# F in tiles of 64x64 instead of 32x32, its blocks put in order by the copies, in an RWKV-7 and feed-forward kernel

## The chip, the cores and the metric

The kernel runs on one core of a Trainium2 chip. The metric is the device time of one execution in microseconds; the time before is the median of eight runs, 871.92 us (868.44 to 874.09). Lower is better. Engines are named as in the profile: PE (TensorE matmul), PEld (its weight loads), DVE (VectorE), ACT (ScalarE), POOL (GpSimd), SP (SyncE, which issues nearly all DMAs). Times "at 289.78" are microseconds from the start of the profiled execution's span, and L450 is line 450 of the kernel.

## What is computed

Two blocks, one after the other, in fp32. The first is a recurrence over 768 tokens for 4 batches x 8 heads, with a 40 x 40 state for each; the second is a feed-forward layer over the 3072 resulting rows:

```python
for t in range(S):                       # r, k, v, w, a, b: (4, 8, 768, 40)
    y[:, :, t] = np.einsum('bhd,bhde->bhe', rt, state)
    Sa = np.einsum('bhde,bhe->bhd', state, at)
    state_decay = state * wt[:, :, None, :] - np.einsum('bhd,bhe->bhde', Sa, bt)
    state = state_decay + np.einsum('bhd,bhe->bhde', vt, kt)
x = y.transpose(0, 2, 1, 3).reshape(3072, 320)
h = x @ w_in                             # 320 -> 2048
out = (h * np.clip(h + 3.0, 0.0, 6.0) / 6.0) @ w_out
```

## The kernel before, in words

**Units.** The recurrence is worked off in blocks of 64 tokens. A unit is one such block for two batches (two halves of 64 partitions, `q`) and all eight heads (four pairs `pr` of two heads `s`). There are 24 units; four of them (`NU`) make a group. A unit's work is split into stages, each a small generator: first it issues matmuls or transposes on PE, then yields, then issues what reads the PSUM result.

**Stages that prepare a unit** (`prepare`, L389): W (decay, L391, then the scan on DVE), gam (reciprocals and copies of the running products), A and B (transposes of a and b, scaled into `at` and `bt`), F (L438, the products of `at` and `bt` within the block), K, factor (L458: four transposes of the decay on PE, the ACT copy `rgt` at L465, two POOL products `KBt` at L473), E (products of `kt` and `at`) and EV. **Stages that carry the state** (`step`, L594): RT, VT, S (transposes), R (L619, at times state), U (L653), UT (L674), rS (L690), C, sn (L708), H, y (L731), move.

**F and the inversion.** F holds, for each batch and head, a 64 x 64 matrix of which two 32 x 32 diagonal blocks and one off-diagonal block are used. It is written per unit to a tile for the whole group (`F`, 128 partitions x 32 heads x 64). The lower 32 rows of each half hold their two column blocks in exchanged order, so that both diagonal blocks lie in columns 0 to 31. When the group's fourth unit has its F (units 7, 11, 15, 19, 23), `invert` (L526) begins: one DVE transpose `fb` (L531) of columns 0 to 31 of the whole group, a masking on POOL (`x`, L534), then 30 pairs of DVE instructions (L543 and L549, forward substitution), two DVE transposes (L552, L556) and copies to `tinv`. It is handed out in small steps between other work (`aside`). `third_block` (L565) then makes the off-diagonal blocks from rows 32 to 63 and columns 32 to 63 of F, two units at a time.

**F's two steps before.** PE: 32 matmuls with 32 columns of weights (40 x 32) and 64 columns of data, each placed on an array tile of 64 rows x 32 columns; for the lower rows (`c` = 1) the data are read with exchanged halves. ACT: two copies of 128 partitions x 256 elements with factor -1 (L456). A matmul in fp32 is two records in the profile, so F shows as 64.

**PSUM.** The recurrence has a ring of five banks of 128 x 512 (`any`); `ps_any` takes the next one, and a pair of results (`ps_pair`, one for each `s`) takes two, which later stages share while columns are left. The feed-forward part has two banks `h` and one `o`. A bank is taken again only when all that reads it has been done.

**The order of the work** is written out by hand; each engine runs its queue in that order. From unit 4 on, the main loop (L1062) goes through four blocks per unit. `a_block` (L1031) collects the stages due in a block: those of the unit that carries the state (`OWN_STAGES`) and those of units being prepared ahead (`AHEAD_STAGES`, or `CLOSE_STAGES` where the next unit begins less than four blocks later, as in units 8 to 11; there, factor stands in the same block as F, otherwise one block later). `begins` (L1028) sets when units are begun: unit 8 in block 0, then 9, 10 and 11 three blocks apart, from 12 on four apart. `together` (L998) issues the PE parts of the collected stages in the order `PRODUCTS` (factor early, F last) as long as five banks suffice, then the parts that read them in the order `RESULTS`, in which F stands ahead of factor. Between the two halves of a block, `feed` gives out pieces of the feed-forward stream: `expand` (L806 and L811 on PE, relu on ACT at L816, the product `gt` on DVE at L817) and `contract` (L830 on PE, the output copy `ob` at L848).

Of the kernel before, what the change touches and what calls it, by code (L numbers as in the profile page):

```python
# [12 lines left out]
AF = mybir.ActivationFunctionType  # L13
# [3 lines left out]
P = 128  # L17
BL = 64
HB = BL // 2
L = 32  # L20
# [3 lines left out]
def _ap(ap, extra, dims):  # L24

    return bass.AP(tensor=ap.tensor, offset=ap.offset + extra, ap=[list(ap.ap[0])] + dims)
# [3 lines left out]
def kernel(  # L30
# [42 lines left out]
    nc = tc.nc  # L73
    B, H, T, D = r.shape
    NG = T // (2 * BL)
    NPR = H // 2
    NP = B // 2
    NU = 2 * NP
# [21 lines left out]
    def ps_any(shape):  # L100
        tag, bufs = ring[0]
        ring.rotate(-1)
        return bank(tag, shape, bufs)
# [4 lines left out]
    def ps_pair(*dims):  # L108

        n = 1  # L110
        for d in dims:
            n *= d
        if shared[0] is None or shared[1] + n > 512:
            shared[:] = [ps_any([P, 512]) for _ in range(2)], 0
        at = shared[1]
        shared[1] += n
        views, step = [], n
        for d in dims:
            step //= d
            views.append([step, d])  # L120
        return [_ap(t[:], at, views) for t in shared[0]]
# [6 lines left out]
        out=ident[:], in_=ones, pattern=[[1, P]],  # L128
# [4 lines left out]
        out=ones[:, 0:BL], in_=ones[:, 0:BL], pattern=[[1, BL]],  # L133
# [3 lines left out]
        out=ones[BL:P, 0:BL], in_=ones[BL:P, BL:P], pattern=[[1, BL]],  # L137
# [34 lines left out]
    start = const.tile([P, SCAN], F32, name="start")  # L172
# [12 lines left out]
    for i in range(3):  # L185
        t = const.tile([P, H, BL], F32, name=f"score{i}")
# [14 lines left out]
    for p in range(NP):  # L201
        t = const.tile([P, 2, NPR, SLOT], F32, name=f"state{p}")
        nc.vector.memset(t[:], 0.0)
        state.append(t)
        t = const.tile([P, 2, NPR], F32, name=f"last{p}")
# [113 lines left out]
    PE, DONE = 1, 2  # L319
# [46 lines left out]
    def half(i, n=SLOT):  # L366
        return slice(SLOT * i, SLOT * i + n)
# [21 lines left out]
    def prepare(i, F):  # L389
        n, o = i % NU, data[i]  # L390
# [44 lines left out]
            bt = o["bt"] = turned("bt")  # L435
            nc.vector.tensor_tensor(out=bt[:], in0=x[:], in1=o["rg"][:], op=ALU.mult)

        def f_stage():  # L438

            f = ps_pair(NPR, BL)  # L440
            for pr in range(NPR):
                for c in range(2):
                    for q in range(2):
                        for s in range(2):
                            x = q * BL + c * L
                            y = o["bt"][half(s, D), pr, half(q)].rearrange("p (c t) -> p c t", c=2)
                            if c:
                                y = y[:, ::-1, :]
                            z = (q ^ s) * BL + c * L
                            nc.tensor.matmul(out=f[s][z:z + L, pr, :],  # L450
                                             lhsT=o["at"][half(s, D), pr, x:x + L], rhs=y,
                                             start=True, stop=True, tile_position=(s * SLOT, z))
            yield PE
            for s in range(2):
                x = n * H + 4 * s
                nc.scalar.activation(out=F[:, x:x + 4, :], in_=f[s], func=AF.Copy, scale=-1.0)  # L456

        def factor_stage():  # L458

            rg = ps_any([P, NPR, P])  # L460
            for pr in range(NPR):
                nc.tensor.transpose(out=rg[:, pr, :], in_=o["rg"][:, pr, :], identity=ident[:])
            yield PE
            rgt = tmp.tile([P, H, D], F32, name="rgt", bufs=RGT)
            nc.scalar.activation(  # L465
                out=rgt[:], in_=rg[:].rearrange("p r (s e) -> p (r s) e", s=2)[:, :, 0:D],
                func=AF.Copy,
            )
            t = grp.tile([P, HD + WPAD], F32, name="KBt", tag="KBt", bufs=NU + 2)
            nc.gpsimd.memset(t[:, 2 * HD:], 0.0)  # L470
            for x, name in enumerate("KB"):
                o[name] = t[:, x * HD:x * HD + WPAD]
                nc.gpsimd.tensor_tensor(  # L473
                    out=o[name][:, 0:HD].rearrange("p (h e) -> p h e", h=H),
                    in0=o[name + "N"][:, :, 0:D], in1=rgt[:], op=ALU.mult,
                )
            if i > 2 * NU:
                fetch("V", i)
            for name in "BK":
                fetch(name, following(i))  # L480
# [12 lines left out]
        def ev_stage():  # L493
# [10 lines left out]
            for q in range(2):  # L504
                for s in range(2):
                    nc.scalar.activation(out=EV[half(q ^ s), s], in_=ev[q][half(q ^ s)], func=AF.Copy)
            o["EV"] = EV

        return {"W": w_stage, "gam": gam_stage, "A": a_stage, "B": b_stage, "F": f_stage,
                "factor": factor_stage, "K": k_stage, "E": e_stage, "EV": ev_stage}  # L510

    def in_turn(stages, order):
# [375 lines left out]
    third, F, group_F = [], None, []  # L888

    def prepared(i):  # L890
        nonlocal F
        if i >= NK:
            return None
        if i % NU == 0:
            F = inv.tile([P, NH, BL], F32, name="F", tag="F", bufs=2)
            group_F.append(F)
        return prepare(i, F)
# [223 lines left out]
```

## Time and profile before

| | |
|---|---|
| median of 8 runs | 871.92 us (868.44 to 874.09) |
| the profiled execution | 871.94 us, of which its span 870.2 |
| mean granted PE clock | 0.932 of full speed |
| PE busy, of 870.2 | 787.3 us |
| DVE, ACT, POOL busy | 535.7, 288.8, 150.9 us |
| F's matmuls, L450 | 1536 records, 64 in each unit |
| F's copies, L456 | 48, 390 ns each (median) |

The last 1.7 us of the profiled execution's time lie outside the span. In the profile's time lines a row gives the start, the length from the first start to the last end, the engine, line, operation, output <- inputs, the shape, and how many instructions were merged into the row; in brackets stand the engine's idle time ahead of it and the releaser, where there is one. Because matmuls overlap, the pace of PE is read from the start of one row to the start of the next. The profile's stretches give busy time per engine between two times, and the granted clock (1.00 is full speed).

### The profile page before, as it was taken

The numbers are of one execution on the slowest core, as the hardware profiler recorded it, in microseconds if no ns is written. First come the engines' busy times: TensorE is split into PE (matmuls) and PEld (weight loads), VectorE is DVE, ScalarE is ACT, GpSimd is POOL, SyncE is SP. The second block draws the span as 40 slices with busy tenths as digits, with TensorE's granted clock in tenths as the row PEclk, the third lists the DMA queues.
The fourth block names the chain that finished last, engine by engine and source line by source line (L and its number), as shares of the span: only waits on it lengthen the run. The fifth ranks groups of instructions, "written<-read, shape, count | busy, mean of one in ns | idle before, by whom it ended". The sixth has DMA issues, their size and how long they took to land.

```text
span 870.2 us, 36251 instructions
## 1 busy us (share of the span) xinstructions
PE 787.3 (90%) x16128; PEld 671.3 (77%) x16128; DVE 535.7 (62%) x1141; ACT 288.8 (33%) x694; POOL 150.9 (17%) x295
## 2 busy tenths in 40 slices
PE   4710988798999999999999999999999999999998
PEld 3610876686888788887888888788888888888886
DVE  7999678878845579833679543787445774221211
ACT  1334744232333322432323433223342224322211
POOL 4221011122111130220221122112212202000000
PEclk8655568998999999999999999999999999999999
DMA  6543434431122331322221232221232101110000
GB/s 132 89 109 94 114 105 106 71 65 33 30 50 52 62 56 30 56 44 40 50 49 37 46 53 51 39 51 31 46 59 42 26 19 27 22 24 13 18 17 15
DMA packets 175979, 45.08 MB, mean 52 GB/s; under 512 B 157904, under 2 KB 173264, under 8 KB 175824
## 3 DMA queue, kind: packets, MB, share of 16 engines
q1 hardware_dynamic: 174768, 42.61, 25.2%
q8 instruction: 127, 2.08, 1.0%
q10 hardware_dynamic: 1056, 0.16, 0.1%
q14 instruction: 28, 0.23, 0.1%
HBM read 34.08 MB, written 3.93 MB: 44 GB/s over the span
## 4 chain that ended last, share of the span: by engine, by line
PE 69%; DVE 6%; issue 2%; SPq 2%; ACT 1%; POOL 1%; DMA 0%; DVEq 0%
PE o L830 22%; PE h L806 18%; PE h L811 5%; PE any L358 5%; PE any L376 3%; PE any L708 2%; PE any L731 2%; PE any L450 2%; DVE x L549 1%; DVE prod L543 1%; PE any L619 1%; PE any L584 1%; PE any L653 1%; PE any L572 1%; PE any L690 1%
## 5 line engine op out<-in xcount | busy, mean ns | idle before, releaser
L830 PE MATMUL o<-wout,gt 128*128 128x320 f32 x768 | 232.4, 448 | 0.8 <-issue 0.6
L806 PE MATMUL h<-xt,win 128*128 128x128 f32 x1536 | 196.8, 281 | 0.6 <-DVE gt L817 0.6
L806 PEld LDWEIGHTS h<-xt,win 128*128 128x128 f32 x1536 | 185.0, 194 | 10.5 <-DVE gt L817 1.4
L830 PEld LDWEIGHTS o<-wout,gt 128*128 128x128 f32 x768 | 140.0, 191 | 56.0 <-issue 2.5
L817 DVE SCALAR_TENSOR_TENSOR gt<-gt,h 128x512 f32<-128x512 f32 x96 | 61.5, 682 | 110.5 <-ACT gt L816 110.5
L816 ACT ACTIVATE gt<-h,three 128x512 f32<-128x512 f32 x96 | 60.8, 685 | 159.5 <-PE h L811 159.4
L741 POOL TENSOR_TENSOR yg<-ys,gam 128x512 f32<-128x512 f32 x24 | 41.4, 1724 | 220.8 <-DVE ys L738 148.3
L543 DVE TENSOR_TENSOR prod<-x 128x30 f32<-128x30 f32 (+9 forms) x180 | 63.5, 353 | 11.7 <-POOL x L534 6.9
L549 DVE TENSOR_TENSOR x<-x,prod 128x30 f32<-128x30 f32 (+9 forms) x180 | 63.0, 350 | 4.3
L473 POOL TENSOR_TENSOR KBt<-K,rgt 128x320 f32<-128x320 f32 x24 | 22.4, 935 | 222.3 <-ACT rgt L465 208.6
L811 PE MATMUL h<-xt,win 64*128 64x128 f32 x768 | 56.2, 286 | 0.0
L385 DVE COPY_PREDICATED score<-mask,any 128x256 f32<-128x256 int32 x143 | 53.0, 434 | 0.0
L811 PEld LDWEIGHTS h<-xt,win 64*128 64x128 f32 x768 | 47.0, 188 | 5.4 <-issue 0.4
L412 DVE RECIPROCAL gam<-prods 128x256 f32<-128x256 f32 x24 | 41.4, 1739 | 13.4 <-POOL yg L741 13.1
L738 DVE TENSOR_TENSOR ys<-any,ys 128x256 f32<-128x256 f32 x48 | 18.2, 420 | 45.5 <-PE any L500 29.3
L715 DVE TENSOR_TENSOR state<-any,state 128x160 f32<-128x160 f32 x48 | 13.2, 316 | 49.6 <-PE any L376 49.4
L427 DVE RECIPROCAL rgam<-prods 128x256 f32<-128x256 f32 x24 | 41.8, 1741 | 0.0
L401 DVE TENSOR_TENSOR_SCAN prods<-wm,start 128x528 f32<-128x528 f32 x24 | 30.1, 1254 | 17.1 <-ACT wm L398 15.5
L572 PE MATMUL any<-tb,F 32*32 32x32 f32 x768 | 16.0, 199 | 26.7 <-DVE tb L552 26.3
L267 ACT ACTIVATE parts<-parts,low 128x256 uint32<-128x256 uint32 x40 | 20.3, 508 | 56.8 <-DVE parts L265 56.6
L572 PEld LDWEIGHTS any<-tb,F 32*32 32x32 f32 x768 | 14.6, 115 | 29.5 <-issue 27.9
L605 ACT ACTIVATE RT<-any 128x512 f32<-128x512 f32 x24 | 14.3, 596 | 65.9 <-PE any L358 65.9
(136 smaller groups left out, 1181.7 us busy)
## 6 DMA issues: line engine op xcount, KB each, us to landing
raw<-in_moe_w_out_dram SPq DMA_DIRECT2D x20, 256.0 KB
B<-in_b_dram SPq DMA_DIRECT2D x48, 80.0 KB
K<-in_k_dram SPq DMA_DIRECT2D x48, 80.0 KB
V<-in_v_dram SPq DMA_DIRECT2D x96, 40.0 KB
R<-in_r_dram SPq DMA_DIRECT2D x96, 40.0 KB
out_dram<-ob SPq DMA_DIRECT2D x48, 80.0 KB
W<-in_w_dram SPq DMA_DIRECT2D x40, 80.0 KB
A<-in_a_dram SPq DMA_DIRECT2D x40, 80.0 KB
```

Of the source, the lines that this page charges most:

```text
L358: nc.tensor.transpose(out=o[:, n, :], in_=x[:, 2 * n:2 * n + 2, :].rearrange("p s e -> p (s e)"), identity=ident[:])
L385: nc.vector.copy_predicated(out=x[:, 4 * i:4 * i + 4, :], mask=mask4, data=o[i])
L412: nc.vector.reciprocal(gv[:, :, 0:HB], o["prods"][:, :, 0, 1:HB + 1][:, :, ::-1])
L427: nc.vector.reciprocal(rv[:, :, HB:BL], o["prods"][:, :, 1, 1:HB + 1])
L543: nc.vector.tensor_tensor(out=pv, in0=_ap(x[:], (i + 1) * L + i, [[L, n], [0, i]]), in1=_ap(x[:], i * L, [[0, n], [1, i]]), op=ALU.mult,)
L549: nc.vector.tensor_tensor(out=rest, in0=rest, in1=pv, op=ALU.add)
L741: nc.gpsimd.tensor_tensor(out=yg[:], in0=m["ys"][:].rearrange("p r q t -> p r (q t)"), in1=o["G"][:], op=ALU.mult)
L806: nc.tensor.matmul(out=hp[c][:, i, :], lhsT=win[:, t, j * P:(j + 1) * P], rhs=xt[:, t, :], start=(t == 0 and i == 0), stop=False)
L811: nc.tensor.matmul(out=hp[c][:, i, :], lhsT=win2[half(c), (j0 + i) * P:(j0 + i + 1) * P], rhs=xt[half(c), 2, :], start=False, stop=(i == N ...
L816: nc.scalar.activation(out=gt[:], in_=hp[c][:], func=AF.Relu, bias=three[:], scale=1.0)
L817: nc.vector.scalar_tensor_tensor(out=gt[:], in0=gt[:], scalar=6.0, in1=hp[c][:], op0=ALU.min, op1=ALU.mult)
L830: nc.tensor.matmul(out=op[:], lhsT=gts[c][:, n, :], rhs=wout[:, c * HJ + r * NQ + n, :], start=((split or r == 0) and c == 0 and n == 0), ...
```

## The change

From the ninth unit on (units 8 to 23, `i >= 2 * NU`) F is made by 16 matmuls with 64 columns of weights on array tiles of 64 x 64, with the data read in their own order. The exchange of the lower rows' column blocks is done by the copies instead: for each `s` and each half, one copy of the upper 32 rows, columns 0 to 31 only (32 partitions x 128 elements), and one of the lower 32 rows with the two blocks of 32 columns exchanged (32 partitions x 256 elements). So the two copies become eight. Columns 32 to 63 of the upper rows are no longer written; nothing reads them. Units 0 to 7 keep the old form, now called `f_by_32`.

```diff
-        def f_stage():
+        def f_by_32():
...
+        def f_by_64():
+
+            f = ps_pair(NPR, BL)
+            for pr in range(NPR):
+                for q in range(2):
+                    for s in range(2):
+                        nc.tensor.matmul(out=f[s][half(q ^ s), pr, :],
+                                         lhsT=o["at"][half(s, D), pr, half(q)],
+                                         rhs=o["bt"][half(s, D), pr, half(q)],
+                                         start=True, stop=True)
+            yield PE
+            for s in range(2):
+                x = n * H + 4 * s
+                for z in range(0, P, BL):
+                    nc.scalar.activation(out=F[z:z + L, x:x + 4, 0:L], in_=f[s][z:z + L, :, 0:L],
+                                         func=AF.Copy, scale=-1.0)
+                    y = f[s][z + L:z + BL].rearrange("p r (c t) -> p r c t", c=2)
+                    nc.scalar.activation(
+                        out=F[z + L:z + BL, x:x + 4, :].rearrange("p h (c t) -> p h c t", c=2),
+                        in_=y[:, :, ::-1, :], func=AF.Copy, scale=-1.0)
...
-        return {"W": w_stage, "gam": gam_stage, "A": a_stage, "B": b_stage, "F": f_stage,
+        return {"W": w_stage, "gam": gam_stage, "A": a_stage, "B": b_stage, "F": f_by_32 if i < 2 * NU else f_by_64,
```

## The prediction

> **What bounds the kernel now.** I read the page first (busy shares, then the chain that ended last), then busy time by stretches, then the instructions in order of time around the sixteen F stages that change.
>
> ```profile
> PE 787.3 (90%) x16128; PEld 671.3 (77%) x16128; DVE 535.7 (62%) x1141; ACT 288.8 (33%) x694; POOL 150.9 (17%) x295
> ...
> PE 69%; DVE 6%; issue 2%; SPq 2%; ACT 1%; POOL 1%; DMA 0%; DVEq 0%
> ```
>
> The chain is mostly TensorE (PE), so PE time taken away is time gained, wherever PE doesn't wait. The stretches say where that is (columns: stretch, its length, then busy us of PE, PEld, DVE, ACT and POOL, granted clock, DMA):
>
> ```profile
> 244.00:356.00 112.00, 109.01 (x2510) 92.55 (x2507) 74.29 (x146) 36.66 (x93) 22.61 (x44) 1.00 0.29 51
> 356.00:870.00 514.00, 506.75 (x10208) 432.69 (x10208) 258.05 (x527) 160.09 (x375) 80.04 (x141) 1.00 0.19 36
> ```
>
> The changed units 8 to 23 have their F matmuls (L450) at 247.7, 269.3, 288.9, 308.6 and 335.8 (units 8 to 12) and from 369.6 to 676.1 (units 13 to 23). From 356 on PE has hardly any idle time, and the chain is PE throughout. From 316 to 356 the chain runs through VectorE (DVE): the first of the later inversions is pressed into that time, and PE waits for DVE at 324.41 (0.77 us) and at 356.00 (0.42 us). So a gain of PE counts in units 8 to 11 (unless a new wait eats it) and 13 to 23, and is worth nothing in unit 12.
>
> **What the matmuls give.** F goes from 32 matmuls of 32 columns of weights to 16 of 64 (each is two records, 64 and 32). The same shape runs in E and H (L376) and in rS (L690), so its price is in the trace; unit 15, PE alone:
>
> ```profile
> 425.41 0.67 PE L674 MATMUL any<-tinv,RR 64*64 64x64 f32 x32
> 425.90 0.65 PE L690 MATMUL any<-RT,S 40*64 40x64 f32 x32
> 426.48 0.86 PE L450 MATMUL any<-bt,at 40*32 40x64 f32 x64
> 427.27 2.42 PE L830 MATMUL o<-wout,gt 128*128 128x320 f32 x8
> ...
> 436.31 0.65 PE L376 MATMUL any<-at,kt 40*64 40x64 f32 x32
> 436.89 0.54 PE L830 MATMUL o<-wout,gt 128*128 128x320 f32 x1
> ```
>
> Start to start, a 64-wide block takes 0.49 us before another 64-wide one (425.41 to 425.90) and 0.58 before a change of shape (L690 to L450, L376 to L830); L450 takes 0.79. After rS (units 8 and 12 to 23), L690 and L450 cost 0.58 + 0.79 now and 0.49 + 0.58 then: 0.29 us less (1.37 - 1.07, by unrounded starts). In units 9 to 11 L450 follows 128-wide transposes, and the gain is 0.79 - 0.58 = 0.21. Bounds: nothing, if sixteen matmuls take as long as 32, and 0.30 (0.79 - 0.49). I take 0.29 and 0.21, by the rows of the same shape. On the path: 11 x 0.29 = **3.2 us** in units 13 to 23, 0.29 in unit 8, none in unit 12.
>
> **What the copies cost.** Two ScalarE (ACT) copies of 128 x 256 become eight of 32 partitions, four of 128 elements and four of 256 (reversed halves; L397, reversed too, takes as long as L398, so that is free). Two rows say how such copies follow each other:
>
> ```profile
> 330.65 1.11 ACT L506 ACTIVATE EV<-any 64x160 f32<-64x160 f32 x4 [2.23 <-PE any L500]
> ...
> 335.46 0.50 ACT L658 ACTIVATE U<-any 128x160 f32<-128x160 f32 x2 [0.47 <-PE any L674]
> ```
>
> Both are 160 elements, 0.30 us each. L658 starts its second after 0.50 - 0.30 = 0.20. L506 has three steps in 1.11 - 0.30 = 0.81: its second step stays on the same partitions (0.20), the first and third go from one half to the other: (0.81 - 0.20) / 2 = 0.305, the whole duration. So copies overlap by 0.1 us only where the first partition stays. The new eight change it every time (0, 32, 64, 96, twice). Durations by the line through 160 (0.298) and 256 elements (0.390): 0.268 for 128. Sum: 4 x 0.280 + 4 x 0.402 = **2.73 us** until ACT is free, against 0.54 now. Bounds: all overlapping, 4 x (0.17 + 0.264) = 1.73; all as dear as a 256-element one, 8 x 0.402 = 3.2. I take 2.73, as those rows change partitions too.
>
> The Trainium skill, "ScalarE: Activation LUTs", section "What ACT_TABLE_LOAD costs", gives 186 ns + 0.833 ns per element for an ACTIVATE with immediate scale and bias, and lets back-to-back ones overlap by about 93 ns. By it the eight take 2.02 us (an estimate), and the whole sum below would end at 870.3; the L506 row speaks against the overlap here.
>
> ACT is 33% busy, so most of these 2.2 extra us are hidden: in units 13 to 23 the next ACT instruction is due 0.8 to 6.3 us after F's end, or is an output copy (L848) whose bank is next needed several us later; the E matmuls that reuse F's PSUM banks come 3.9 us or more after F's end. The shortest (units 18 and 22, 0.8 us) delay the relu L816 by 0.9 us, and its bank is not written for 10 us. In unit 8 F would end at 251.5, and the E matmuls that take its bank come at 252.7. In units 15, 19 and 23 DVE's transpose fb (L531) waits for F, with gt, state and masks queued behind it; they come 1 to 2 us late, and PE asks for them 3 us later or more. Without these covers each unit would lose up to 1.9 us net.
>
> **Where they are not hidden: units 9 to 11.** There the weights' transposes (L462) and F share a round of the five PSUM banks, and rgt (L465) is queued on ACT behind F's copies. PE's next pair of banks includes rgt's. Unit 10:
>
> ```profile
> 289.78 0.66 ACT L456 ACTIVATE F<-any 128x256 f32<-128x256 f32 x2 [3.36 <-PE any L450]
> 290.32 0.44 ACT L465 ACTIVATE rgt<-any 128x320 f32<-128x320 f32 x1
> ...
> 291.40 0.68 PE L619 MATMUL any<-state,at 40*64 40x40 f32 x32
> ```
>
> F's first copy moves to 289.78 - 0.21 = 289.57, rgt starts 2.73 later and ends at 292.74, so L619 starts at 292.78: 1.38 late. Unit 9 the same way: copies from 270.16 - 0.21, rgt to 273.12, L653 at 273.16, not 272.25: 0.91 late. Both are on the chain. Unit 11 starts the inversion:
>
> ```profile
> 310.25 2.18 DVE L531 STREAM_TRANSPOSE fb<-F 128x1024 f32<-128x1024 f32 x1 [1.30 <-ACT F L456]
> 313.80 0.20 DVE L543 TENSOR_TENSOR prod<-x 128x30 f32<-128x30 f32 x1 [1.37 <-POOL x L534]
> ...
> 315.24 0.48 DVE L610 TENSOR_TENSOR state<-state,scale 128x320 f32<-128x320 f32 x1
> 316.03 0.76 DVE L738 TENSOR_TENSOR ys<-any,ys 128x256 f32<-128x256 f32 x2 [0.30 <-PE any L731]
> ```
>
> fb starts at 309.35 + 2.72 + 0.03 = 312.10, 1.85 late; DVE's queue behind it has 0.30 of slack at L738, and from there to 356 DVE has no other: 1.55 late. PE then waits for DVE.
>
> **Sum**, against the profiled execution (871.94, a span of 870.2 and 1.7 around it; the median of the runs, 871.92, is the same): -0.29 + 0.91 + 1.38 + 1.55 = +3.55 by 356, then -3.19: +0.36. **872.3 us.**
>
> **Rivals.** (1) Copies overlap: 1.73 instead of 2.73 makes units 8 to 11 -0.29 - 0.09 + 0.38 + 0.68 = +0.68, and with -3.19 the time is 869.4. For it: the same-partition rows; against it: L506. (2) A PE stall goes: at 398.46 in unit 14, in the middle of L450, PE stops for 1.41 us with nothing shown to wait for ("issue"), and then runs at half clock; the denser bursts of small matmuls seem to provoke it (another 0.30 at 588.38, in unit 20's L450). Fewer records may spare it: 1.41 + 1.8 (next rival) off, 869.1. Against: it can as well fall elsewhere. (3) Slower, by the clock: after that 1.41 us the granted clock was 0.50 from 402 to 404, and 16 L806 took 3.18 instead of 1.78, 16 L811 1.48 instead of 1.09: 1.8 us. My own sum opens a PE gap of 292.78 - 291.19 = 1.6 us in unit 10 and one of 0.77 + 1.55 + 0.21 = 2.5 at 324. The point from which it decides is a gap somewhere about 1.4: 1.30 at 297.88 left the clock at 1.00. Once: 874.1; the second costs 1.8 less the 0.7 of slack before 356: 875.2. Against: gaps of 2.15 near 160 kept the clock. (4) The change doesn't give what it says, the block of sixteen taking 0.79: 876.4 (3.55 + 0.29 + 3 x 0.21). Against: four blocks of that very shape in every unit.
>
> The Trainium skill, "TensorE: Matmul & The Clock Gate", section "Why this matters for your kernels", sees the clock fall only after idle gaps of about 3 us; by it rival 3 would cost nothing. The 1.41 us row disagrees.
>
> "TensorEngine Tiling (Array Packing)", section "PSUM Bottleneck", speaks against the change: it asks to vectorize PSUM access across tiles of a bank, as copies may become the bottleneck; eight for two is the reverse, and no sum here needs it.
>
> **Numbers.** Forecast 0.40 (870.6 to 873.7), rival 1 0.12, rival 2 0.22, rival 3 0.21, rival 4 0.05. 0.2% is 1.7 us, about what a measurement can tell from no change: faster 0.34, same 0.40, slower 0.26. The range takes in 869.1 and 874.1 with the dearer copies (8 x 0.402 adds 0.47 in each of units 9 to 11) and half of rival 3's second gap: 868.6 to 875.0.
>
> **What would show it.** Per unit: L450 x32 in 0.49 to 0.58 start to start; eight F copies in about 2.7 us without overlap; L653 and L619 of units 9 and 10 waiting for ACT rgt; fb 1.8 us later against its L450; a longer gap at 324; PE dense after 356. Wrong: copies at 0.17 and 0.26 steps, no rgt wait, half clock after the new gaps, or PE idle after 356.

## The result, and the profile after

The changed kernel takes **866.49 us** (median of 17 runs, 864.04 to 869.7) against 871.71 us for the kernel before (47 runs, 867.96 to 875.11). The ratio is 0.9941, with a 95% interval of 0.993 to 0.9953: 5.2 us, 0.6%, faster. The forecast was 872.3 us, and 866.49 lies below its range (868.6 to 875.0). The profiled execution took 865.83 us, of which its span is 864.1 (before: 871.94 and 870.2).

In the changed kernel's line numbers everything behind F is 21 higher: L464 is the new F matmul, L472 and L475 are its copies (128 and 256 elements), and rgt, fb, the R matmul, U, UT and rS are L486, L552, L640, L674, L695 and L711. From the page, busy time and the chain:

```profile
PE 782.0 (90%) x15616; PEld 668.2 (77%) x15616; DVE 536.4 (62%) x1141; ACT 318.1 (37%) x790; POOL 151.6 (18%) x295
...
PE 70%; DVE 6%; issue 2%; ACT 1%; DMA 1%; POOL 0%; SPq 0%; DVEq 0%
```

PE has 512 records and 5.3 us of busy time less, ACT 96 copies and 29.3 us more. The chain is PE's as before, so the copies as a whole are hidden. The stretches tell where the 6.1 us of the span went. They are cut at about the same work in both kernels (near the start of the U matmuls of units 4, 8 and 19), and hold the length, then the busy us of PE, PEld, DVE, ACT and POOL, the granted clock and DMA. Before:

```profile
245.00:368.00 123.00, 119.59 (x2762) 102.16 (x2760) 83.85 (x161) 43.77 (x109) 25.90 (x50) 1.00 0.29 52
368.00:709.00 341.00, 338.26 (x7313) 291.08 (x7312) 207.23 (x418) 113.27 (x275) 65.78 (x116) 0.99 0.24 44
```

After:

```profile
245.00:369.00 124.00, 118.39 (x2601) 101.17 (x2600) 83.64 (x161) 53.22 (x139) 25.87 (x50) 1.00 0.28 51
369.00:703.00 334.00, 332.85 (x6964) 287.13 (x6962) 209.49 (x419) 133.29 (x341) 65.91 (x116) 1.00 0.25 45
```

In the first stretch, which holds F of units 8 to 12, the changed kernel loses 1 us: PE has 1.2 us less work and waits 2.2 us more. In the second, with F of units 13 to 23, it gains 7 us: 5.4 us less PE time, and 1.6 us less PE idle time. By unrounded starts of the same instructions:

| us | up to unit 4's U | units 8 to 12 | units 13 to 23 | rest of PE's work |
|---|---|---|---|---|
| before | 245.08 | 122.96 | 341.31 | 156.12 |
| after | 245.20 | 124.11 | 333.94 | 156.12 |
| difference | 0.12 | 1.15 | -7.37 | 0.00 |
| by the forecast's steps | 0 | 3.55 | -3.19 | 0 |

So both stretches came out better than forecast: the first by 2.4 us, the second by 4.2. The table is made of one profiled execution of each kernel.

**PE's part, as forecast.** Unit 15, PE alone in the changed kernel:

```profile
424.66 0.65 PE L711 MATMUL any<-RT,S 40*64 40x64 f32 x32
425.12 0.65 PE L464 MATMUL any<-bt,at 40*64 40x64 f32 x32
425.70 2.42 PE L851 MATMUL o<-wout,gt 128*128 128x320 f32 x8
```

From rS to F it is 0.46 us and from F to the output matmuls 0.58: 1.04 against 1.37 before. The forecast was 1.07. In units 9 to 11 the block takes 0.63 instead of 0.79, which gives 0.16 and not the 0.21 of the forecast.

**The copies, as forecast.** ACT in unit 10, and what stands behind the copies:

```profile
289.68 0.27 ACT L472 ACTIVATE F<-any 32x128 f32<-32x128 f32 x1 [3.23 <-PE any L464]
289.96 0.38 ACT L475 ACTIVATE F<-any 32x256 f32<-32x256 f32 x1
...
292.38 0.44 ACT L486 ACTIVATE rgt<-any 128x320 f32<-128x320 f32 x1
```

The eight take 0.267 and 0.375 us, and the next one starts 0.28 and 0.39 us after its predecessor's start: no overlap, and 2.67 us from the first start to the last end, where 2.73 had been forecast until ACT is free.

**rgt's wait, not as forecast.** The forecast had the R pair that PE takes after F of unit 10 start behind rgt, at 292.78. PE there:

```profile
291.27 0.68 PE L640 MATMUL any<-state,at 40*64 40x40 f32 x32
```

It starts at 291.27, a microsecond before rgt starts, and waited for nothing. Behind F of unit 9, where the forecast had the U pair wait for rgt too, it waits 0.32 us, for the last copy of F:

```profile
272.51 0.61 PE L674 MATMUL any<-RR,tinv 64*64 64x40 f32 x27 [0.32 <-ACT F L475]
```

**The late fb, as forecast.** DVE in unit 11:

```profile
311.90 2.21 DVE L552 STREAM_TRANSPOSE fb<-F 128x1024 f32<-128x1024 f32 x1 [3.08 <-ACT F L475]
...
317.32 0.75 DVE L759 TENSOR_TENSOR ys<-any,ys 128x256 f32<-128x256 f32 x2
```

fb starts at 311.90, 1.65 us later than before; the forecast had 312.10. The slack of 0.30 that L738 (now L759) had is gone, and PE's stop at 324 is 2.35 us long where 2.5 had been forecast. At 357 PE waits for DVE for 0.73 us (before: 0.42 at 356.00).

**PE's stops that wait for nothing shown.** Before, in unit 14 (the stop the second rival spoke of):

```profile
397.64 0.82 PE L450 MATMUL any<-bt,at 40*32 40x64 f32 x60
399.87 0.30 PE L450 MATMUL any<-bt,at 40*32 40x64 f32 x4 [1.41 <-issue]
```

Before has four of over 0.25 us behind 245: 1.41 with half clock behind it (3.2 us in all, by the time from one unit to the next), 0.40, 0.63 and 0.30. All four are gone, with some 5.2 us. After has one that is new, in unit 13:

```profile
370.76 0.64 PE L464 MATMUL any<-bt,at 40*64 40x64 f32 x31
372.55 0.27 PE L464 MATMUL any<-bt,at 40*64 40x64 f32 x1 [1.15 <-issue]
```

It costs 1.25. So these stops give the changed kernel's profile some 3.9 us, more than the matmuls themselves (0.32 per unit, 3.5 us in units 13 to 23).

**What the stops have in common.** All records of PE's queue are counted, from 0 and in order of start: matmuls, weight loads, and the queue's own records, which a time line of PE does not show (before: 434 semaphore waits and 3 drains; after: 440 and 3). The first matmul behind the stop is then record 14273, 17601, 20930 and 22210 in before, and 12482 in after. Divided by 256 these leave 193, 193, 194, 194 and 194. By matmuls and weight loads alone the remainders would show nothing. The part of the page on DMA queues, before:

```profile
q8 instruction: 127, 2.08, 1.0%
```

The same line of the changed kernel says 123 packets and 2.02 MB: four packets fewer for 1018 records fewer (1024 matmuls and weight loads, 64 in each of 16 units, less 6 semaphore waits more). One packet of 16 KB thus brings about 256 records, and the stops' places repeat with 256. That PE stops where the next packet isn't there in time is the theory that the second half of the experiments tests. It predicts that a stop depends on where a dense burst of small matmuls falls in the stream, so that records added far ahead of it move or remove it.

### The profile page after: what moved, and what is told of

It reads as the page before. It is cut to its first block, busy times and chain, and to the rows that moved or that the text cites. A ratio compares the mean times of both kernels' runs of the same rounds, so it can differ in the third digit from the quotient of the medians.

```text
span 864.1 us, 35329 instructions
## 1 busy us (share of the span) xinstructions
PE 782.0 (90%) x15616; PEld 668.2 (77%) x15616; DVE 536.4 (62%) x1141; ACT 318.1 (37%) x790; POOL 151.6 (18%) x295
## 3 DMA queue, kind: packets, MB, share of 16 engines
q8 instruction: 123, 2.02, 1.0%
## 4 chain that ended last, share of the span: by engine, by line
PE 70%; DVE 6%; issue 2%; ACT 1%; DMA 1%; POOL 0%; SPq 0%; DVEq 0%
PE o L851 23%; PE h L827 19%; PE any L358 5%; PE h L832 5%; PE any L376 3%; PE any L729 2%; PE any L752 2%; DVE x L570 1%; DVE prod L564 1%; PE any L640 1%; PE any L674 1%; PE any L593 1%; PE any L605 1%; PE any L711 1%; PE any L695 1%
## 5 line engine op out<-in xcount | busy, mean ns | idle before, releaser
L564 DVE TENSOR_TENSOR prod<-x 128x30 f32<-128x30 f32 (+9 forms) x180 | 65.4, 363 | 12.9 <-POOL x L555 8.1
L759 DVE TENSOR_TENSOR ys<-any,ys 128x256 f32<-128x256 f32 x48 | 18.1, 419 | 39.1 <-PE any L521 23.3
```

The source lines that it names most:

```text
L564: nc.vector.tensor_tensor(out=pv, in0=_ap(x[:], (i + 1) * L + i, [[L, n], [0, i]]), in1=_ap(x[:], i * L, [[0, n], [1, i]]), op=ALU.mult,)
```

## The experiments

**Theory and rivals.** Theory T: the matmuls give 0.3 us a unit; the copies cost only the late fb of unit 11; the rest of the gain is that F's fewer records shift the stream, so that dense bursts meet the packets' boundaries elsewhere. Rival S: it is the shape, since matmuls of 32 columns provoke the stops and those of 64 do not. Rival M: the stops are chance, and differ between executions.

Runs 1 to 4 share their runs of the kernel before (871.55 us, 867.7 to 875.2), runs 5 to 8 another set (870.24, 868.2 to 873.08); 9 and 10 are single runs, with one run of the kernel before beside them (873.53). The recorded expectations name their own theories A and B.

**1. The copies alone.** The matmuls of 32 columns stay, with data in their own order; the eight copies as in the change.

```diff
...
+                for c in range(2):
+                    for q in range(2):
+                        for s in range(2):
+                            x = q * BL + c * L
+                            z = (q ^ s) * BL + c * L
+                            nc.tensor.matmul(out=f[s][z:z + L, pr, :],
+                                             lhsT=o["at"][half(s, D), pr, x:x + L],
+                                             rhs=o["bt"][half(s, D), pr, half(q)],
+                                             start=True, stop=True, tile_position=(s * SLOT, z))
```

> 32 matmuls of 32 columns as before, but with the data in their own order, and the eight copies. Theory A (the gain is PE time plus stalls of PE's instruction stream that happen to be gone; the copies cost only where someone waits for them): the PE stream has as many instructions as before, so its stalls stay; unit 9's U matmuls wait for F's last copy (270.16 + 2.67 against 272.25: +0.6) and the inversion's first transpose in unit 11 comes 2.0 us late with 0.3 of slack (+1.7): 2.3 us slower than before, about 874. Theory B (reading the data with exchanged halves, or the 32-column tiles themselves, make the stalls and the lost time): the order alone would already give something back, and the time is at or below that of before, 869 to 872.

Measured: 876.01 us (873.97 to 879.35), ratio 1.0051 (1.0031 to 1.0071): 4.5 us slower than before. Its PE waits from 240 on (in total, times, longest):

```profile
PE any L467 <- issue: 3.0, 3, 1.5
PE any L643 <- DVE score L385: 2.3, 1, 2.3
```

The wait for DVE is the late fb, as in the changed kernel. Units 8 to 12 take 125.01 us against 122.96 before: the copies cost 2.0 us there. Units 13 to 23 take 340.36 against 341.31. The three stops (1.48, 1.03 and 0.44 us) lie at 403, 555 and 591, which are records 14273, 20930 and 22210, as in before; the fourth place, 17601, has none of over 0.25 us. Behind the first the clock stayed at 1.00, so there this profile is 1.6 us better than before's. With as many F records as before, three of the four stops stay. In the profile 2.8 us of this kernel's 3.9 us lie ahead of 245, where the two programs are the same; why is open (see the end of this section).

**2. The matmuls alone.** Sixteen matmuls of 64 columns, the two old copies; the exchange of the lower rows' blocks is left out.

```diff
-                for z in range(0, P, BL):
...
+                nc.scalar.activation(out=F[:, x:x + 4, :], in_=f[s], func=AF.Copy, scale=-1.0)
```

> 16 matmuls of 64 columns, but the two old copies; the exchange of the lower rows' blocks is left out, so the inversion works on other numbers. Theory A: without the eight copies the wait of unit 9 (0.32) and unit 11's late transpose (1.6) go, and the rest of the change stays: 1.9 us below the changed kernel, about 864.6. Theory B: as the copies are hidden, the same as the changed kernel, 866.5. PE's idle time at 324 should be back to 0.8 to 1.0 us (A) or stay at 2.35 (B).

Measured: 862.79 us (860.95 to 867.48), ratio 0.9906 (0.9874 to 0.9938). Units 8 to 12 take 121.94 us, units 13 to 23 332.68. The stop at 324 is 0.78 us, unit 9 has no wait, and no stop without a shown cause is longer than 0.15 us. Against the changed kernel's profile the copies thus cost 124.11 - 121.94 = 2.2 us in units 8 to 12; 0.3 of it is the wait in unit 9. From 13 on the difference is 1.26, of which the stop at 371 makes 1.0 by the time from one unit to the next and a delay at another such boundary, in unit 14, 0.2: nothing is left for the copies there. That they are hidden in units 13 to 23 is shown.

**3. Unit 11 in the old form.**

```diff
-"F": f_by_32 if i < 2 * NU else f_by_64,
+"F": f_by_32 if i < 2 * NU or i == 11 else f_by_64,
```

> The changed kernel, but unit 11 (the one whose F starts the first of the later inversions) with the old F. Theory A: its transpose comes as early as before, 1.6 us gained, 0.2 of PE lost: 865.1; PE's instruction stream is 64 records longer from there on, so stalls may move by a us or two either way. Theory B (the gap at 324 is slack that costs nothing): 866.5 to 866.8.

Measured: 863.39 us (861.29 to 864.51), ratio 0.9903 (0.9878 to 0.9928). DVE:

```profile
307.89 2.17 DVE L552 STREAM_TRANSPOSE fb<-F 128x1024 f32<-128x1024 f32 x1 [1.21 <-ACT F L456]
```

fb waits 1.21 us for F instead of 3.08, and PE's stop behind it is 0.77 us. Units 8 to 12 take 122.69, 1.4 us less than in the changed kernel (124.11), which is the late fb's price as forecast (1.55). Units 13 to 23 take 332.96, and the one stop is 0.42 us. This version beats both kernels: its interval lies below that of the changed kernel's ratio (0.993 to 0.9953). Of the 3.1 us between the medians the traces thus show 1.4 for the late fb and 1.0 in units 13 to 23, where the stop is smaller; the rest is not accounted for.

**4 to 8. The same work, shifted in the stream.** To separate place from shape, PE's stream is lengthened far ahead: in unit 3, before 245 and ahead of a stretch of 26 us in which PE is idle, the last matmul of EV is issued n times more into the same PSUM place (4n records). Nothing behind it changes but its place in the stream. Runs 4, 5 and 6 do this to the kernel before, with n = 32, 16 and 48; runs 7 and 8 to the changed kernel, with n = 16 and 48.

```diff
+            if i == 3:
+                for _ in range(32):
+                    nc.tensor.matmul(out=ev[q][half(q ^ s), pr, :], lhsT=o["E"][half(q), 4 * s + pr, :],
+                                     rhs=VN[half(q), 4 * s + pr, 0:D], start=True, stop=True)
```

> The kernel before with unit 3's last EV block issued two more times over (32 extra matmuls, 128 records), written just ahead of the long PE idle time of 26 us at 55, so that nothing but the place of the later PE instructions in the stream moves. Theory A (PE now and then runs out of fetched instructions, where depends on the place in the stream, and the half clock after the stop of 1.41 us is part of the price): the stops at 398, 485, 553 and 588 move or go, and the time differs from that of before by more than 1 us, most likely down to 867 to 870. Theory B (the stops belong to the 32-column blocks, wherever they lie in the stream): 871.7 within 0.7, with stops again in L450's blocks.

> The kernel before with 16 extra matmuls (64 records) ahead of the idle time at 55. Theory A (stops belong to the place of PE's instructions in the stream, which repeats with each 16 KB fetched): stops elsewhere, the time anywhere from 866 to 872, and each us of it after 245 accounted for by stops and by half clock after them. Theory B (the 128 records of e4 did something else, in the first stage, and the time falls with the number of extra records): about 870.

> The kernel before with 48 extra matmuls (192 records). Theory A: as above, 866 to 872, not in order of the number of extra records. Theory B: less than e4, about 866.7.

> The changed kernel with 16 extra matmuls (64 records) ahead of the same idle time. Theory A: it has only 1.15 us of stops, so it can gain 1.2 us at most or lose up to 5: 865 to 871. Theory B (the changed kernel keeps its time wherever its stream lies, as the dense bursts are shorter): 866.5 within 1.

> The changed kernel with 48 extra matmuls (192 records). Theory A: 865 to 871; the mean of the changed kernel over the shifts lies below that of the kernel before by what the parts without stops give, 2.3 us. Theory B: 866.5 within 1, and the mean over the shifts differs by 3.5 us or more.

Measured, with the stops of over 0.25 us behind 245 and their records:

| kernel, n | us | ratio (95%) | units 13 to 23 | stops, us at record (left over by 256) |
|---|---|---|---|---|
| before, 0 | 871.71 | 1 | 341.31 | 1.41 at 14273 (193), 0.40 at 17601 (193), 0.63 at 20930 (194), 0.30 at 22210 (194) |
| before, 16 | 868.55 | 0.9985 (0.9971 to 0.9999) | 340.43 | 1.40 at 18370 (194), 0.43 at 25281 (193) |
| before, 32 | 868.33 | 0.9958 (0.9939 to 0.9976) | 336.60 | 0.32 at 12994 (194) |
| before, 48 | 875.25 | 1.0045 (1.0026 to 1.0064) | 339.79 | 1.12 at 12994 (194), 1.41 at 26561 (193) |
| after, 0 | 866.49 | 0.9941 (0.993 to 0.9953) | 333.94 | 1.15 at 12482 (194) |
| after, 16 | 863.41 | 0.9932 (0.9909 to 0.9955) | 332.38 | none |
| after, 48 | 869.91 | 0.9992 (0.9974 to 1.001) | 333.01 | 0.28 at 14017 (193) |

The same F stage of unit 14, in before with n = 32:

```profile
399.21 0.86 PE L450 MATMUL any<-bt,at 40*32 40x64 f32 x64
400.00 2.05 PE L810 MATMUL h<-xt,win 128*128 128x128 f32 x16
```

The same 64 records in the same order, on the same work, run without a stop once they lie 128 records further on. That speaks against rival S. That each stop lies at 193 or 194 of 256, in every kernel, speaks against rival M. Unit by unit, run 4 and run 2 differ by 0.32 us in units without a stop, 3.5 us in eleven: that is the matmuls' share. The rest of what the profiles of the plain kernels differ by in units 13 to 23 is the stops. Averaged over these places, the stretch takes 339.5 us before (four programs) and 333.1 after (three). That is 6.4 us, not 3.5: at these places the changed kernel doesn't only have its stops elsewhere, it has fewer, 0.48 us of them in a program against 1.86. With three and four places that mean is rough.

Not all of this was expected. Run 6 lies above its 866 to 872 and run 7 below its 865 to 871. The mean of the ratios is 0.9997 for the four programs of before and 0.9955 for the three of after, 3.7 us apart, where theory A of run 8 had 2.3; its theory B, each within 1 us of 866.5, fails with 863.41 and 869.91.

The medians follow the stops only in part. The kernel before with n = 48 is 0.45% slower than plain, though its profile from 245 on is 1.7 us shorter (618.73 against 620.39 us); the changed kernel with n = 48 took 250.52 us up to 245's place in its profile, where plain takes 245.20. What varies there is told at the end of this section.

**9. As many records as before, in the new shape.** Each of F's 16 matmuls is issued twice, so that the stream is as long as before and the shape is that of the change.

```diff
...
+                        for _ in range(2):
+                            nc.tensor.matmul(out=f[s][half(q ^ s), pr, :],
+                                             lhsT=o["at"][half(s, D), pr, half(q)],
+                                             rhs=o["bt"][half(s, D), pr, half(q)],
+                                             start=True, stop=True)
```

> The changed kernel with each of the 16 F matmuls issued twice (same result), so that PE's stream has as many records as before, at the same places, but in 64-column blocks. Theory A (a stop comes where a boundary of 256 records falls into a burst of small matmuls; in the kernels run so far every stop without a shown wait lies at record 193 or 194 of 256): stops, if any, at the records of the kernel before (14273, 17601, 20930, 22210), that is in units 14, 17, 19 and 20, shorter, as the burst takes 0.3 us longer; units 13 to 23 take 332.4 + 11 x 0.49 = 337.8 us and the stops. Theory B (the 32-column blocks make the stops): none, 337.8.

One run: 876.92 us, beside 873.53 for the kernel before. Its PE waits from 330 on:

```profile
PE any L465 <- issue: 1.7, 2, 0.9
```

L465 is its F matmul, of 64 columns. The stops are 0.91, 0.37 and 0.76 us, at records 14273, 17601 and 20930: the very places where the kernel before stops. So matmuls of 64 columns stop too, and rival S is out. Units 13 to 23 took 342.60 us, where 337.8 and the stops were expected; 1.3 us of the excess are the doubled block, which takes 1.19 us start to start and not 1.07. Behind the stop at 324 (2.29 us, the late fb) the clock fell to half for 6.8 us, and units 8 to 12 took 128.93 us.

**10. The copies reordered,** so that two copies in succession start at the same partition: for each of the two halves first the small copies of both `s`, then the large ones.

```diff
-            for s in range(2):
-                x = n * H + 4 * s
-                for z in range(0, P, BL):
+            for z in range(0, P, BL):
+                for s in range(2):
+                    x = n * H + 4 * s
...
+                for s in range(2):
+                    x = n * H + 4 * s
```

> The changed kernel with the eight copies reordered, so that two in a row begin at the same partition (s innermost). If copies overlap only where the first partition stays, four of eight steps get 0.11 us shorter: first copy to last end 2.2 us instead of 2.67, the transpose fb 0.45 earlier in unit 11, the gap at 324 at 1.9 instead of 2.35; unit 10's R then waits 0.3 for the seventh copy. If the order doesn't matter: 2.67, 2.35 and no wait in unit 10. The time moves by less than its runs scatter; the trace decides.

One run: 869.2 us (873.53 for the kernel before). ACT in unit 10:

```profile
291.69 0.42 ACT L472 ACTIVATE F<-any 32x128 f32<-32x128 f32 x2 [3.23 <-PE any L464]
292.13 0.64 ACT L477 ACTIVATE F<-any 32x256 f32<-32x256 f32 x2
```

Two copies that start at the same partition take 0.42 and 0.64 us, by a step of 0.17 and 0.28 from one start to the next; to a copy with another start partition the step is 0.26 and 0.37. All eight take 2.17 us instead of 2.67, as the forecast's reading of L506 has it. In this order the last copy of F's s=0 is the seventh, and R in unit 10 now waits for it:

```profile
293.28 0.98 PE L642 MATMUL any<-state,at 40*64 40x40 f32 x29
...
294.13 0.68 PE L376 MATMUL any<-RT,VT 40*64 40x64 f32 x31
```

R's first matmuls (s=0) start at 293.28; the first of s=1 starts at 293.65, 0.05 us behind the end of that copy and ahead of rgt, which starts at 293.89. From R to the next block it takes 0.85 us, in the changed kernel 0.49. The one stop without a shown wait (0.85 us, at 375) lies at record 12482, as in the changed kernel, whose stream of PE this run shares: the place repeats from one execution to another. The stop at 324 shrinks to 1.85, but behind it the clock fell, which the same stretch of the changed kernel didn't show. Here the reordered kernel (granted clock third from the end):

```profile
328.00:332.00 4.00, 3.62 (x67) 3.00 (x68) 3.73 (x11) 0.00 (x0) 0.00 (x0) 0.59 0.26 62
```

and the changed kernel, the same work:

```profile
326.00:330.00 4.00, 3.50 (x77) 3.00 (x78) 3.73 (x12) 0.44 (x1) 0.00 (x0) 1.00 0.23 55
```

Units 8 to 12 thus take 125.43 us, more than the changed kernel's 124.11, in spite of the shorter copies. With one run, whether the order of the copies gains anything stays open.

**What the packets show.** The traces keep the time of every packet of the instruction queue. Numbered from 1, packet k belongs to the boundary at record 256 k + 193: at all 19 stops the last packet to land ahead of PE's restart is the one of that number. Some of them, and one boundary without a stop:

| kernel, record | packet starts | lands | PE goes on | after the landing |
|---|---|---|---|---|
| before, 14273 | 397.27 | 398.68 | 399.87 | 1.19 |
| before, 20930 | 551.03 | 552.30 | 553.63 | 1.33 |
| after, 12482 | 369.70 | 371.10 | 372.55 | 1.45 |
| run 9, 14273 | 400.98 | 402.02 | 403.44 | 1.42 |
| before, 23745, no stop | 620.66 | 621.78 | 623.03 | 1.24 |

In all 19 stops PE goes on 1.19 to 1.48 us after the landing, and at none of the 1179 boundaries behind 245 in the twelve programs does the record start earlier than 1.19 us after it. So it is the packet that PE waits for: where the stream comes to the boundary later than that, it runs through. Two things decide how it falls out, how fast the records ahead are issued and how early the packet was started. Ahead of the stop at 398, 256 records took 1.76 us and the packet had been started 149 records before; at 623 they took 1.82 us, but the packet had been started 294 before, and PE was just in time. Over all these boundaries the lead lies between 51 and 299 records.

**What stays open.** The time up to unit 4's U, in which F is the same in all kernels, was between 241.4 and 250.5 us in the twelve profiled executions; the spread within one kernel's runs (7 us for before) is of that size. This is why the medians are read with their intervals, and the causes in the stretches behind it. Nor is it shown what sets the moment at which a packet is started, and so which of the dense boundaries become stops.

## Why the prediction was wrong

Right, by its own steps:

- *The matmuls.* 0.29 us a unit forecast, 0.32 measured, and in units 9 to 11 0.21 and 0.16; 3.2 us in units 13 to 23 forecast, 3.5 measured.
- *The copies.* 2.73 us forecast, 2.67 measured, without overlap; rival 1 (1.73) is out. They are hidden from unit 13 on, as run 2 shows. The rule of the Trainium skill, "ScalarE: Activation LUTs", section "What ACT_TABLE_LOAD costs", of an overlap of about 93 ns does not hold where the start partition changes (steps of 0.28 for 0.267 us) and does where it stays (0.17 for 0.267).
- *Unit 11.* fb 1.85 us later forecast, 1.65 measured; the loss of 1.55 came out as 1.58, by PE's stop of 2.35 instead of 0.77 (1.4 in run 3).

Wrong:

- **"PE's next pair of banks includes rgt's"** (units 9 and 10), +0.91 and +1.38 in the sum. Behind F of unit 10 the R pair waits for nothing, and behind F of unit 9 the U pair for 0.32 us, on F's last copy and not on rgt. I had counted the banks off as a ring that is gone through in turn, as the section on PSUM above has it. They aren't. The program's own waits behind F of unit 10 show it (the numbers count an engine's instructions):

```
R, s=0: the bank that K used; waits for DVE 508 (kt)
R, s=1: the bank of F, s=0;   waits for ACT 286 (the last copy of F, s=0)
rgt itself is ACT 291
```

  F's s=0 is read by the first four copies, done at 291.01, before R is due at 291.27. Run 10 confirms it: once the seventh copy is the last to read that bank, R's s=1 waits for the seventh. At both places the pair gets banks whose last readers end ahead of rgt in the trace (kt at 289.30, F's two at 291.01 and 292.35, rgt at 292.81 in unit 10); by what rule the pool chooses, no run here shows. Behind F of unit 9 the U pair takes both F banks (it waits for ACT 259 and 263), and the second is read by the last copy: hence 0.32. Units 8 to 12 lost 1.15 us instead of 3.55, and 2.25 of these 2.4 us are this step: at the R pair of unit 10 the changed kernel stands 0.25 us ahead of before, counted from unit 4's U, where the forecast's terms had it 2.0 behind (-0.29 + 0.91 + 1.38). Before the change the trace couldn't tell the two readings apart, since both banks were free in time.

- **The second rival, left out of the sum.** The sum put PE's stops at nothing. The rival was given 3.2 us and a chance of 0.22, with the remark that the stop can as well fall elsewhere. The stop at 398.46 did go, with half clock behind it; three more of before went too, and one new one came: 3.9 us net. It belonged in the sum with a mean and a spread. The profile of before already held what was needed: four stops at the same place of 256 records, and 1024 records to be taken out of the stream. I read two of the four, and put them down to the density of the burst. Density alone doesn't decide; the place does, as run 4 shows. Which stops would go and which would come that profile does not tell, as the packets' start times vary.

- *Rival 3* (half clock behind the new stops) did not happen in the changed kernel's profile, but in runs 9 and 10 it did, behind 2.29 and 1.85 us. Its point "somewhere about 1.4" is not one: 2.35 us (after), 1.48 us (run 1) and 1.41 us (run 6, at 674) kept the clock at 1.00, 1.41 us (before) and 1.40 us (run 5) lost it. The Trainium skill, "TensorE: Matmul & The Clock Gate", section "Why this matters for your kernels", speaks of idle gaps of about 3 us; here shorter ones were followed by half clock too.

- *Rival 4* is out: the block of sixteen takes 0.58, not 0.79.

In sum, in the profiled executions: +0.36 forecast, less 2.4 in units 8 to 12 (2.25 of it the banks), less 3.9 for the stops, less 0.3 for the matmuls' size gives -6.2; measured from 245 on: 614.17 against 620.39, -6.2.

## What to carry to other kernels

Before a wait for a PSUM bank is put into a sum, find out from the program which bank is handed out next: here it was not the next in turn, and a count in turn gave 2.3 us of waits where there were 0.3. Where a profile shows short stops of PE without a releaser, count the records of PE's queue up to each, semaphore waits included: if they fall on one remainder of 256, any change in the number of matmuls moves them, and an effect of half a per cent has to be averaged over a few such shifts before it is put down to the change itself. When one instruction is split into several, look for the one place where its end is awaited: leaving unit 11 in the old form took 1.4 us off units 8 to 12, for 0.16 us of PE time in that unit.

## What the runs showed of the hardware that was not expected

- All 19 stops of PE of over 0.25 us without a shown wait, behind 245 in the twelve programs, lie at record 193 or 194 of 256, and one instruction packet of 16 KB is about 256 records. They are 0.28 to 1.48 us long, and PE goes on 1.19 to 1.48 us after a packet has landed. Records added ahead, with nothing else changed, moved the median by -0.4% to +0.45%.
- Half clock followed PE stops of 1.40, 1.41, 1.85 and 2.29 us, but not others of 1.41, 1.48 and 2.35: length alone doesn't decide.
- ACT copies from PSUM overlap by 0.1 us if they start at the same partition and not at all if they don't: 0.17 against 0.28 us for 32 x 128, 0.28 against 0.39 for 32 x 256.
